# Loading x by channel halves in a long convolution by FFT: two alternating tiles, pieces behind the inverse evictions

## The chip, the cores and the metric

One Trainium2 chip, of which one core is used. The metric is the device time of one execution in microseconds (us). Three runs of the kernel before took 2089.24, 2091.68 and 2093.18 us; their median is 2091.68 us. One more execution was taken with the hardware profiler; all lines of the profile come from it.

A core has five engines, each with a queue of its own that runs in order: PE (matrix products; its weight loads are shown as PEld), DVE, ACT and POOL (elementwise work) and SP (it only issues transfers here). DMA transfers are issued from SP, ACT or POOL and run on 16 DMA engines that all of them share. A transfer that converts f32 to a 16 bit type is issued from POOL in this kernel.

## The reference

```python
def _attn_ref(x, h):                       # x: (8, 5696, 128), h: (5696, 128)
    L = 2 * S
    Xf = np.fft.rfft(x, n=L, axis=1)
    Hf = np.fft.rfft(h, n=L, axis=0)
    y = np.fft.irfft(Xf * Hf[None, :, :], n=L, axis=1)[:, :S, :]
    return y
def _moe_ref(x, w_theta, w_tok_r, w_tok_i, w_ch):
    theta = x @ w_theta
    zr, zi = x * np.cos(theta), x * np.sin(theta)
    y = einsum('ts,bsd->btd', w_tok_r, zr) + einsum('ts,bsd->btd', w_tok_i, zi)
    u = x + y
    return u + np.maximum(u @ w_ch, 0.0)
# reference(...) = _moe_ref(_attn_ref(x, h), ...)
```

A causal convolution over 5696 positions, for 8 batches and 128 channels, is computed by a Fourier transform of length 11392. Its result goes through a phase, two products with matrices of 5696 x 5696, and a channel product.

## The kernel before

The convolution comes first and ends some 420 us into the span; then two passes of products with the big matrices follow, with the weights streamed through a ring of six buffers (`load_w`, line 517, POOL), transposed by DVE (line 722) and multiplied by PE (line 1107).

The transform is split in two factors, 64 by 178 (`N2`, `N1`); 178 of real input needs `K1` = 90 frequencies. One *group* is two batches and 64 of the 128 channels (`HD`): `groups` has 8 of them, `(bp, dh)` with the batch pair `bp` 0 to 3 and the channel half `dh` 0 or 1, `dh` running fastest. A group goes through four stages:

- **Stage a** (`stage_a`, 16 chunks): four matmuls a chunk (line 195) with x as weights, then one eviction from PSUM to the tile `a`, on ACT (line 202; 0.69 us).
- **Stage b** (`stage_b`, 12 chunks, called forward chunks): `f2` (line 213) does the second factor with the table `w_t2`; ACT evicts to `xs` (line 310; 0.97 us); DVE multiplies by the spectrum of h into `uv` (lines 312 and 317; 1.23 us). The spectrum comes in tiles `hs` from `hf_hbm` (`load`, line 303, issued by SP): four buffers, so four chunks are loaded ahead and the others are issued as a product releases a buffer. After the last chunk 12 warm-up matmuls run (line 219).
- **Stage c** (`stage_c`, 16 chunks, the inverse's first factor): 16 matmuls a chunk (lines 333, 334), evicted to the tile `g`, mostly by DVE (line 341; 1.22 us), some by ACT (lines 338, 339).
- **Stage d** (`stage_d`, 7 chunks, the inverse's second factor): matmuls with `g` (line 356), evicted to `yt` by ACT or DVE (lines 362, 360), then stored to `yt_hbm` by SP (line 371).

All PSUM tiles of these stages come from one pool of four.

`woven` sorts the steps of several lists by a position between 0 and 1 and so fixes the order in which each engine gets them; a list spread from w0 to w1 has its step i of n at w0 + (i + 0.5)/n (w1 - w0). The loop over groups (from line 610) does two weaves for each group g. The first has stage c of g, stage a of g+1 and the first four `hs` loads of g+1. The second has stage b of g+1 and stage d of g. In the first, stage a lies between 0 and 0.35 when g has `dh` 0 and between 0 and 0.55 when it has `dh` 1; stage c lies between 0.06 and 1.

x is loaded by `load_x(bp)` (line 122): both channel halves of a batch pair at once, f32 to f16, in 16 transfers from POOL (line 131): for each of two batches and four ranges of 16 rows, one of 80 partitions and one of 9. There is one tile `x16` (pool `fft_x`, one buffer, row pitch `XP` = 132 elements). So the load of the next pair can go out when stage a of the second half has read the tile; `next_x` is put behind stage a in the first weave of each group with `dh` 0. The first pair is loaded at the start (line 234).

Before the groups, h is transformed the same way (lines 231 to 259). Meanwhile the tables are built in pieces: for 15 frequencies of `w_t2` at a time, `w_table` takes an iota and a scaling on POOL (lines 151, 153, two buffers), rounding on DVE (lines 156, 157, 164) and two sines on ACT (lines 161, 168). The pieces from 0, 15 and 30 are made before `load_x(0)`, those from 45, 60 and 75 after it. The h chunks 5 to 11 (`h_chunk`; evictions on line 247 for odd ones, on line 249 for even ones) need the later pieces. Then come the tables `r` (lines 276, 277), the signs (line 290) and `e`, also from POOL by way of DVE and ACT.

After the first weave of the seventh group, `xin` is closed: x's memory goes to the phase stage, and POOL loads `w_theta`, `w_ch` and the tile `ya` (lines 534 and 550), used from the last group's first weave on.

Of the kernel before, what the change touches and what calls it, by code (L numbers as in the profile page):

```python
# [12 lines left out]
F16 = mybir.dt.float16  # L13
# [9 lines left out]
def kernel(  # L23
# [10 lines left out]
    nc = tc.nc  # L34
    B, S, D = x.shape
    assert D == 128
    P = 128
# [39 lines left out]
    N2 = 64  # L77
    N1 = NF // N2
    NB = S // N2
    K1 = N1 // 2 + 1  # L80
    CK = 8
    HD = D // 2
    EN = N2 // 2 + 1
    WARM = 12
    XP = D + 4
    assert N1 * N2 == NF and NB * N2 == S and NB % 2 == 1 and K1 <= P
    CHK = [(c0, min(CK, K1 - c0)) for c0 in range(0, K1, CK)]
    NCK = len(CHK)
# [12 lines left out]
    conv, setup, xa, xin, pha = (ExitStack() for _ in range(5))  # L101

    def pool(name, bufs, stack, **kw):
        return stack.enter_context(tc.tile_pool(name=name, bufs=bufs, **kw))

    fa = pool("fft_a", 1, xa)
    fh = pool("fft_h", 4, xa)
    fx = pool("fft_x", 1, xin)
    NE, WB, BT = 9, 6 * 4 * CJ * 64, 7 * 1024
    keep = pool("keep", 1, ctx, side="right")  # L110
    fc = pool("fft_c", 1, conv, side="right")
# [8 lines left out]
    for p0, p1 in ((0, 80), (80, NB)):  # L120
        nc.gpsimd.dma_start(u_t[p0:p1, :N2 * D],
                            bass.AP(tensor=h.tensor, offset=h.offset + p0 * N2 * D,
                                    ap=[[N2 * D, p1 - p0], [1, N2 * D]]))

    def load_x(bp):
        x16 = fx.tile([P, 2, N2, XP], F16, tag="x16", name="x16")
        for e in range(2):
            src = x[2 * bp + e]
            for n0 in range(0, N2, 16):
                for p0, p1 in ((0, 80), (80, NB)):  # L130
                    nc.gpsimd.dma_start(  # L131
                        x16[p0:p1, e, n0:n0 + 16, :D],
                        bass.AP(tensor=src.tensor, offset=src.offset + (p0 * N2 + n0) * D,
                                ap=[[N2 * D, p1 - p0], [D, 16], [1, D]]))
        return x16

    lane = fc.tile([P, 2], F32)
    for p0 in (0, 64):
# [47 lines left out]
    def stage_a(lhs, both=False):  # L186

        st = {}

        def chunk(q):  # L190
            if q == 0:
                st["a"] = fa.tile([P, 2 * K1, HD], F16, tag="a", name="a_")
            ps = psum()
            for i in range(4):
                nc.tensor.matmul(ps[:, i // 2, (i % 2) * 2 * K1:(i % 2 + 1) * 2 * K1], lhs(q + i), f1_t[:NB],  # L195
                                 start=True, stop=True)
            a_out = st["a"][:, :, q:q + 4].rearrange("p k (a q) -> p k a q", a=2)
            a_in = ps[:, :, :4 * K1].rearrange("p a (q k) -> p k a q", q=2)
            if both and q % 8:
                nc.vector.tensor_copy(a_out, a_in)  # L200
            else:
                nc.scalar.activation(a_out, a_in, AF.Copy)
        return [lambda q=q: chunk(q) for q in range(0, HD, 4)], st
# [19 lines left out]
    def woven(*lists):  # L223

        lists = [l if isinstance(l, tuple) else (l, 0.0, 1.0) for l in lists]
        steps = [(w0 + (i + 0.5) / len(l) * (w1 - w0), n, f)
                 for n, (l, w0, w1) in enumerate(lists) for i, f in enumerate(l)]
        for _, _, f in sorted(steps, key=lambda s: s[:2]):
            f()
# [1 line left out]
    for k0 in (0, 15, 30):  # L231
        w_table(k0)
    nc.vector.tensor_copy(h16[:NB], u_t[:NB, :N2 * D].rearrange("p (n h d) -> p h n d", h=2, d=HD))
    x16s = {0: load_x(0)}
    steps, a_h = stage_a(lambda q: h16[:NB].rearrange("p h n d -> p (h n) d")[:, :, q], True)
    woven(steps, [lambda k0=k0: w_table(k0) for k0 in range(45, K1, 15)])

# [106 lines left out]
    def stage_d(st, bp, dh, then=None):  # L344
        def chunk(n0, cn):
            if n0 == 0:
                st["yt"] = fg.tile([P, NB, N2], BF16, tag="yt", name="yt")
            g_, yt = st["g"], st["yt"]
            ps = psum()
            nq = 5 if cn == CN else cn  # L350
            for j in range(cn):
                n = n0 + j
                o = ps[:, j // nq, (j % nq) * NB:(j % nq + 1) * NB]
                for ri in range(2):
                    e_ = e_t[:K1, n, ri, :] if n < EN else e_t[:K1, N2 - n, ri, ::-1]
                    nc.tensor.matmul(o, g_[:K1, ri * N2 + n, :], e_, start=(ri == 0), stop=(ri == 1))
            y_out = yt[:, :, n0:n0 + cn].rearrange("p m (a q) -> p m a q", q=nq)
            y_in = ps[:, :cn // nq, :nq * NB].rearrange("p a (q m) -> p m a q", q=nq)
            if n0 in (0, 3 * CN):
                nc.vector.tensor_copy(y_out, y_in)  # L360
            else:
                nc.scalar.activation(y_out, y_in, AF.Copy)
            if n0 + cn == N2:
                if then is not None:
                    then(yt)
                if then is not None:
                    gate = nc.gpsimd.tensor_copy(small(0, 1)[HD:HD + 1], sides["phases"][1][HD:HD + 1, 3, H - 1:H]).ins
                for e in range(2):
                    t0 = H if then else 0
                    with tc.issue_after(gate) if then else ExitStack():  # L370
                        (nc.gpsimd if then else nc.sync).dma_start(
                            yt_hbm[dh * HD:(dh + 1) * HD, 2 * bp + e, t0:],
                            yt[64 * e:64 * e + 64].rearrange("p m n -> p (m n)")[:, t0:])
        return [lambda n0=n0, cn=cn: chunk(n0, cn) for n0, cn in CHN]
# [4 lines left out]
    def front(g):  # L379
        if g >= len(groups):  # L380
            return [], [], []
        bp, dh = groups[g]
        x16 = x16s[bp].rearrange("p b n d -> p (b n) d")
        steps, a_st = stage_a(lambda q: x16[:NB, :, dh * HD + q])
        return (steps, *stage_b(a_st, dh))

    a0, load0, b0 = front(0)
# [222 lines left out]
    for g, (bp, dh) in enumerate(groups):  # L610
        st = {}
        last = g + 1 == len(groups)
        a_, load_, b_ = front(g + 1)
        if last:
            for _ in range(3):
                steps0.pop(0)()
        now = [with_load(steps0.pop(0), n < 6) for n in range(9)] if last else []
        c_ = stage_c(st, last)
        if dh == 0 and bp + 1 < B // 2:
            def next_x(bp=bp):  # L620
                x16s[bp + 1] = load_x(bp + 1)
            a_ = a_ + [next_x]
        woven((c_, 0.06 if a_ else 0.0, 1.0), (a_, 0.0, 0.35 if dh == 0 else 0.55), now, load_)
        if g + 2 == len(groups):
            xin.close()
            open_phases()
            load_ya0()
        now = [steps0.pop(0) for _ in range(5)] if last else []
        woven(b_, (stage_d(st, bp, dh, load_ya1 if last else None), 0.0, 1.1 if b_ else 1.0), now)
        if g + 2 == len(groups):  # L630
            load_ya1()
            open_ring()
# [56 lines left out]
    bp = cp = wlp = ybp = None  # L689
# [246 lines left out]
    nxt, second, st = None, None, {}  # L936
    ordered = ExitStack()
    for i, (k, p, tt, j0, s0, nj) in enumerate(stretches):
# [13 lines left out]
        if (p, tt, j0 + s0) == (0, 1, 0):  # L952
            with tc.issue_after(sides["late"].ins):
# [4 lines left out]
        woven = (tt is not None and end_of_pair and i + 1 < len(stretches)  # L958
                 and stretches[i + 1][2] is not None)
# [17 lines left out]
        if tt is None:  # L977
            if p:
                aside(True, False)
            if first_of_pair:  # L980
                q = M1 if p else M3
# [188 lines left out]
```

## Time and profile before

| What | Value |
|---|---|
| Profiled execution | 2090.45 us |
| Its span, first to last instruction | 2088.6 us |
| Mean granted TensorE clock | 0.977 |
| PE busy | 1970.4 us (94%) |
| DVE busy | 1589.4 us (76%) |
| POOL busy | 916.2 us (44%) |
| ACT busy | 646.7 us (31%) |
| DMA queue of POOL (software) | 272032 packets, 156.73 MB |
| DMA queue of SP and ACT (hardware) | 176096 packets, 164.05 MB |
| x transfers (line 131) | 32 of 320 KB (9.1 us to landing, median) and 32 of 36 KB (8.2 us) |
| hs transfers (line 303) | 192 of 128 KB, 3.2 us to landing, median |

How to read it. The page gives for each engine its busy time and share of the span. Other views show groups of instructions by source line, the waits of one engine for another, a timeline of one engine, and windows: the busy time of all engines in a stretch of the span, with the number of instructions in brackets, then the granted PE clock (1.00 is full speed), the mean busy share of the DMA engines (over 1 where packets of several queues overlap on one engine) and the GB/s written. In a timeline row stand the start, the duration, engine, line, operation, out<-in and the number of instructions merged, and in brackets the idle time before it with what ended it. A row of the waits has the total time in us, how often, and the longest.

### The profile page before, as it was taken

How to read it: one execution, taken by the hardware profiler on the slowest of the kernel's cores; microseconds unless marked ns; L12 is line 12 of the kernel's file. 1: busy time of each engine (PE TensorE's matmuls, PEld its weight loads, DVE VectorE, ACT ScalarE, POOL GpSimd, SP SyncE). 2: the span in 40 equal slices, each digit the busy share in tenths (PEclk: the TensorE clock that was granted, in tenths of full speed). 3: DMA queues.
4: the chain of work that ended last, by engine and by line, in shares of the span. 5: the costliest groups of instructions: out<-in, count | busy, mean ns of one | idle time of the engine just before them, and what ended most of it. 6: DMA issues, size and time to landing. Idle time of an engine off the chain costs nothing.

```text
span 2088.6 us, 41598 instructions
## 1 busy us (share of the span) xinstructions
PE 1970.4 (94%) x15865; PEld 1084.7 (52%) x15865; DVE 1589.4 (76%) x2809; ACT 646.7 (31%) x979; POOL 916.2 (44%) x1661
## 2 busy tenths in 40 slices
PE   4888989878999999999999999899999999999998
PEld 3687888754444444444444444344444444444444
DVE  7777768876778887888876766876867777777767
ACT  4877867773332323232310000011111111111111
POOL 5302021247444545454566554445353545444450
PEclk8799989999999999999999999999999999999999
DMA  9489595989898989898999899869697878878793
GB/s 142 102 138 172 146 147 164 249 248 244 145 162 172 180 169 168 171 179 171 177 171 163 130 197 258 135 115 154 127 154 128 153 133 146 145 136 151 131 154 86
DMA packets 454312, 334.98 MB, mean 160 GB/s; under 512 B 134823, under 2 KB 407335, under 8 KB 453127
## 3 DMA queue, kind: packets, MB, share of 16 engines
q0 software_dynamic: 272032, 156.73, 56.2%
q1 hardware_dynamic: 176096, 164.05, 27.3%
q10 hardware_dynamic: 5984, 11.54, 1.6%
q8 instruction: 124, 2.03, 0.4%
q14 instruction: 76, 0.62, 0.1%
HBM read 377.11 MB, written 92.49 MB: 225 GB/s over the span
## 4 chain that ended last, share of the span: by engine, by line
PE 65%; DVE 3%; DMA 2%; issue 1%; POOL 0%; ACT 0%; DVEq 0%; POOLq 0%
PE m L1107 61%; DMA ring<-in_moe_w_tok_r_dram 2%; DVE c L1114 1%; DVE b L663 1%; PE utp L802 1%; PE v L809 1%; PE m L1111 1%; DVE wt L722 1%; PE tpz L750 0%; PE theta_ps L404 0%; POOL ring L517 0%; PE m L994 0%; PE m L1028 0%; DMA zl<-zl_hbm 0%; DMA wl<-in_moe_w_tok_i_dram 0%
## 5 line engine op out<-in xcount | busy, mean ns | idle before, releaser
L517 POOL DMA_DIRECT2D ring<-in_moe_w_tok_i_dram x720 | 388.3, 547 | 660.4 <-DVE wt L722 587.5
L517 POOL DMA_DIRECT2D ring<-in_moe_w_tok_r_dram x720 | 386.4, 547 | 148.0 <-DVE wt L722 93.0
L722 DVE STREAM_TRANSPOSE wt<-ring 128x384 f32<-128x384 f32 (+2 forms) x720 | 360.2, 527 | 108.2 <-PE m L1107 70.9
L1107 PE MATMUL m<-b,wt 128*128 128x512 bf16 x1640 | 391.4, 381 | 2.0 <-DVE wt L722 1.7
L1107 PEld LDWEIGHTS <-wt 128*128 128x128 bf16 x1804 | 176.6, 98 | 220.3 <-DVE wt L722 7.5
L1114 DVE TENSOR_TENSOR c<-c,m 128x512 f32<-128x512 f32 x412 | 266.7, 673 | 0.4 <-PE m L1107 0.4
L804 ACT ACTIVATE ring<-utp 128x512 bf16<-128x512 bf16 x85 | 50.7, 597 | 582.1 <-PE utp L802 582.1
L312 DVE TENSOR_TENSOR uv_t<-xs,hs 128x2048 f16<-128x2048 f16 x88 | 105.6, 1224 | 34.9 <-ACT xs L310 20.1
L333 PE MATMUL ps<-r_u,uv_t 128*128 128x128 f16 x1024 | 122.4, 220 | 10.2 <-ACT red L427 3.5
L1028 PE MATMUL m<-b,wt 128*128 128x512 bf16 x480 | 113.9, 387 | 10.8 <-DMA b<-z_hbm 6.3
L131 POOL DMA_DIRECT2D x<-in_x_dram x64 | 48.5, 766 | 167.6 <-PE ps L195 156.7
L334 PE MATMUL ps<-r_v,uv_t 128*128 128x128 f16 x1024 | 121.5, 220 | 0.2
L799 ACT ACTIVATE ub<-c 128x512 bf16<-128x512 f32 x88 | 55.1, 628 | 193.1 <-DMA ring<-in_moe_w_tok_r_dram 114.4
L334 PEld LDWEIGHTS <-uv_t 128*128 128x128 f16 x1024 | 100.3, 98 | 9.3 <-issue 8.1
L333 PEld LDWEIGHTS <-uv_t 128*128 128x128 f16 x1024 | 100.5, 98 | 5.2 <-DVE uv_t L317 3.8
L310 ACT ACTIVATE xs<-ps 128x1024 f16<-128x1024 f32 x96 | 91.2, 986 | 33.1 <-PE ps L213 24.1
L1028 PEld LDWEIGHTS <-wt 128*128 128x128 bf16 x528 | 51.2, 99 | 71.7 <-issue 11.7
L213 PEld LDWEIGHTS <-w_t 64*128 64x128 f16 x3240 | 64.4, 105 | 42.2 <-issue 25.9
L406 ACT ACTIVATE red<-theta_ps,magic 128x512 f32<-128x512 f32 (+1 forms) x46 | 31.6, 687 | 133.1 <-PE theta_ps L404 101.9
L752 ACT ACTIVATE ring<-tpz 128x512 bf16<-128x512 bf16 (+1 forms) x46 | 27.5, 597 | 134.5 <-PE tpz L750 111.7
L428 ACT ACTIVATE mag<-mag,half_pi 128x512 f32<-128x512 f32 (+1 forms) x90 | 65.0, 723 | 0.0
L663 DVE TENSOR_TENSOR b<-b 128x1024 bf16<-128x1024 bf16 x100 | 61.5, 685 | 0.0
(2892 smaller groups left out, 3779.9 us busy)
## 6 DMA issues: line engine op xcount, KB each, us to landing
ring<-in_moe_w_tok_r_dram POOLq DMA_DIRECT2D x352, 96.0 KB, 4.4
ring<-in_moe_w_tok_i_dram POOLq DMA_DIRECT2D x352, 96.0 KB, 5.0
ring<-in_moe_w_tok_r_dram POOLq DMA_DIRECT2D x352, 80.0 KB, 4.3
ring<-in_moe_w_tok_i_dram POOLq DMA_DIRECT2D x352, 80.0 KB, 3.7
hs<-hf_hbm SPq DMA_DIRECT2D x192, 128.0 KB, 3.2
cp_hbm<-c SPq DMA_DIRECT2D x88, 256.0 KB, 2.4
c<-cp_hbm SPq DMA_DIRECT2D x88, 256.0 KB, 3.6
out_dram<-c SPq DMA_DIRECT2D x88, 256.0 KB, 4.2
```

The source lines that it names most:

```text
L213: nc.tensor.matmul(ps[:, e, j * HD:(j + 1) * HD], w_t2[rows, c0 + j, N2 * (1 - ri):N2 * (3 - ri)], a_st["a"][rows, ri * K1 + c0 + j, :], s ...
L310: nc.scalar.activation(xs[:, :, :, :ck], ps, AF.Copy)
L312: nc.vector.tensor_tensor(uv[:, :, :, c0:c0 + ck], xs.rearrange("p e d k -> p e (d k)").unsqueeze(1).to_broadcast([P, 2, 2, HD * CK]), hv. ...
L333: nc.tensor.matmul(o, u_t[:, at:at + P], r_u, start=True, stop=False)
L334: nc.tensor.matmul(o, v_t[:, at:at + P], r_v, start=False, stop=True)
L428: nc.scalar.activation(mag, mag, AF.Sin, bias=half_pi[:m], scale=-TWO_PI)
L517: nc.gpsimd.dma_start(wb[32 * i:32 * i + 32, :ng, :nj * 64], bass.AP(tensor=a.tensor, offset=a.offset + row0 * S + p * H + i * QR + j0 * 6 ...
L663: return [lambda f=f, x=x: f(*x) for f, x in ((nc.vector.tensor_sub, (bt[M3], b12, b22)), (nc.vector.tensor_sub, (bt[M4], b21, b11)), (nc. ...
L722: nc.vector.transpose(wt.rearrange("p j t r -> p (j t r)").bitcast(F32).rearrange("p (j g t) -> p g j t", j=TJ, g=4)[:, :ng, :nj], wb[:, : ...
L1028: nc.tensor.matmul(ms[n // 2 * 2 + h], a[n][:, j, :, r], bts_of[p][jj][n % 2 * 2 + h][:, r, :], start=(n % 2 == 0 and jj == 0 and r == 0), ...
L1107: nc.tensor.matmul(ms[q], a[q][:, j, :, r], bts[jj][q][:, r, :], start=(jj == 0 and r == 0), stop=(jj == NJ - 1 and r == 1 and q not in left))
L1114: nc.vector.tensor_tensor(c, z, ms[q], op=op)
```

## The change

`load_x` now takes a group number. It loads one channel half (64 of 128 channels, rows of 256 bytes in HBM instead of 512) into a tile of half the pitch (`XP` = 66), from a pool of two buffers. It gives back a list of eight pieces, each with a transfer of 80 partitions and one of 9. With `after`, a piece begins with a POOL copy of one element of the tile `g` into the place that the transfer will write, so that the transfer follows the eviction of inverse chunk 2i (element 16i). The pieces for group g+2 are woven into the first weave of group g, from 0.1 to 1.02. At the start the halves of groups 0 and 1 are issued one after the other. Stage a lies between 0 and 0.7 in every group. In the second weave stage d begins at 0.08 instead of 0, which puts its first chunk behind two forward chunks instead of one.

```diff
-    XP = D + 4
+    XP = HD + 2
...
-    fx = pool("fft_x", 1, xin)
+    fx = pool("fft_x", 2, xin)
...
-    def load_x(bp):
-        x16 = fx.tile([P, 2, N2, XP], F16, tag="x16", name="x16")
-        for e in range(2):
+    x16s = {}
+
+    def load_x(g, after=None):
+
+        bp, dh = divmod(g, 2)
+        if g >= B:
+            return []
+        if g not in x16s:
+            x16s[g] = fx.tile([P, 2, N2, XP], F16, tag="x16", name="x16")
+        x16 = x16s[g]
+
+        def piece(i):
+            e, n0 = i // 4, i % 4 * 16
             src = x[2 * bp + e]
-            for n0 in range(0, N2, 16):
-                for p0, p1 in ((0, 80), (80, NB)):
-                    nc.gpsimd.dma_start(
-                        x16[p0:p1, e, n0:n0 + 16, :D],
-                        bass.AP(tensor=src.tensor, offset=src.offset + (p0 * N2 + n0) * D,
-                                ap=[[N2 * D, p1 - p0], [D, 16], [1, D]]))
-        return x16
+            if after is not None:
+                g_ = after["g"]
+                nc.gpsimd.tensor_copy(x16[0:1, e, n0, 0:1], g_[0:1, 0, 16 * i:16 * i + 1])
+            for p0, p1 in ((0, 80), (80, NB)):
+                nc.gpsimd.dma_start(
+                    x16[p0:p1, e, n0:n0 + 16, :HD],
+                    bass.AP(tensor=src.tensor, offset=src.offset + (p0 * N2 + n0) * D + dh * HD,
+                            ap=[[N2 * D, p1 - p0], [D, 16], [1, HD]]))
+        return [lambda i=i: piece(i) for i in range(8)]
...
-    x16s = {0: load_x(0)}
+    for f in load_x(0) + load_x(1):
+        f()
...
-        x16 = x16s[bp].rearrange("p b n d -> p (b n) d")
-        steps, a_st = stage_a(lambda q: x16[:NB, :, dh * HD + q])
+        x16 = x16s[g].rearrange("p b n d -> p (b n) d")
+        steps, a_st = stage_a(lambda q: x16[:NB, :, q])
...
-        if dh == 0 and bp + 1 < B // 2:
-            def next_x(bp=bp):
-                x16s[bp + 1] = load_x(bp + 1)
-            a_ = a_ + [next_x]
-        woven((c_, 0.06 if a_ else 0.0, 1.0), (a_, 0.0, 0.35 if dh == 0 else 0.55), now, load_)
+        woven((c_, 0.06 if a_ else 0.0, 1.0), (a_, 0.0, 0.7), now, load_, (load_x(g + 2, st), 0.1, 1.02))
...
-        woven(b_, (stage_d(st, bp, dh, load_ya1 if last else None), 0.0, 1.1 if b_ else 1.0), now)
+        woven(b_, (stage_d(st, bp, dh, load_ya1 if last else None), 0.08 if b_ else 0.0, 1.1 if b_ else 1.0), now)
```

## The prediction

> **What bounds the kernel now.** The page's chain of waits gives 61% of the span to the matmuls of line 1107, the weight stage after the convolution. None of them changes, so the change is worth what it moves the end of the convolution, which lies in the first 420 us; all that follows starts when its data is there and moves with it. I take the convolution's groups apart by the stretches between their PE landmarks: c(g) runs from the end of one warm-up (line 219) to the next first matmul of line 213, b(g+1) from there to the next warm-up's end. c holds the inverse chunks of group g woven with stage a of group g+1, b the forward chunks of g+1 woven with stage d of g. Windows at these boundaries, c0, b1, c1, b2 and so on:
>
> ```profile
> core 0: us, PE busy (x) PEld busy (x) DVE busy (x) ACT busy (x) POOL busy (x), PEclk, DMA share, GB/s
> 84.54:107.35 22.81, 20.56 (x322) 19.49 (x321) 16.12 (x16) 16.66 (x26) 9.27 (x13) 1.00 0.86 124
> 107.35:129.44 22.09, 16.23 (x499) 14.09 (x498) 16.00 (x14) 14.32 (x16) 2.83 (x4) 0.85 1.26 174
> 129.44:149.34 19.90, 19.90 (x328) 19.64 (x325) 14.63 (x14) 16.46 (x26) 0.00 (x0) 1.00 0.44 122
> 149.34:165.69 16.35, 14.44 (x499) 12.54 (x498) 14.20 (x13) 13.45 (x16) 0.00 (x0) 1.00 0.39 114
> 165.69:189.32 23.63, 21.03 (x328) 19.91 (x326) 15.91 (x15) 17.01 (x27) 8.98 (x12) 1.00 1.06 178
> 189.32:212.37 23.05, 16.94 (x499) 14.93 (x498) 16.13 (x14) 14.38 (x16) 3.00 (x4) 0.85 1.26 168
> 212.37:232.28 19.91, 19.91 (x328) 19.64 (x325) 14.49 (x14) 16.47 (x26) 0.00 (x0) 1.00 0.46 121
> 232.28:248.62 16.34, 14.38 (x498) 12.45 (x497) 14.76 (x13) 13.77 (x16) 0.00 (x0) 1.00 0.39 117
> 248.62:271.23 22.61, 20.81 (x330) 19.82 (x327) 15.34 (x15) 16.54 (x27) 8.84 (x12) 1.00 1.04 179
> 271.23:296.76 25.53, 19.23 (x498) 16.63 (x497) 16.39 (x14) 14.68 (x16) 3.13 (x5) 0.73 1.15 166
> 296.76:316.67 19.91, 19.91 (x328) 19.65 (x326) 14.21 (x13) 16.47 (x26) 0.00 (x0) 1.00 0.42 108
> 316.67:333.01 16.34, 14.52 (x498) 12.52 (x497) 15.02 (x13) 13.76 (x16) 0.00 (x0) 1.00 0.43 124
> 333.01:354.94 21.93, 20.57 (x330) 19.75 (x327) 15.17 (x17) 16.57 (x27) 5.49 (x9) 1.00 0.76 225
> 354.94:371.27 16.33, 14.26 (x498) 12.49 (x497) 14.37 (x13) 13.70 (x16) 0.32 (x1) 1.00 0.55 164
> ```
>
> Two kinds stand out. Three of the b stretches (22.09, 23.05, 25.53) are longer than the other four (16.33 to 16.35), with a DMA share over 1.1 and a granted clock of 0.73 to 0.85 where the others have 1.00. And c with an even group takes 21.93 to 23.63, with an odd one 19.90, in which PE has no gap at all. What DVE waits for in these groups says the first:
>
> ```profile
> DVE uv_t L312 <- ACT xs L310: 14.6, 32, 2.3
> DVE uv_t L312 <- DMA hs<-hf_hbm: 14.3, 10, 3.0
> ```
>
> In the long b stretches the spectra (hs) are late, because the whole next x pair is loaded then: POOL issues it once stage a has read the tile (at 96.6, 178.6 and 260.9), and the last transfer lands some 13 us into b.
>
> **The b stretches, price of the stall.** If x is out of the way they should take 16.34: (22.09-16.34) + (23.05-16.34) + (25.53-16.34) = 5.75 + 6.71 + 9.19 = **21.65 us gained**. The lower clock there goes with it, as it follows the holes in PE.
>
> **The new x load: is it out of the way?** Each group now loads half a pair behind its own inverse evictions. Piece i waits for chunk 2i; by the weave's positions these end near 0.09 + 0.117i of c, so pieces go out every 2.35 us, the last near 19 us into c of 20. The number of rows stays, each is half as long, so the packets double over the kernel. x alone has this rate:
>
> ```profile
> 27.00:32.00 5.00, 3.38 (x120) 3.22 (x120) 4.93 (x7) 2.34 (x3) 4.72 (x8) 1.00 1.70 164
> ```
>
> 164 GB/s written, so a whole pair (2.92 MB in f16) takes 17.8 us when alone. A half load is not in this trace. From below it is 8.9 us (price by bytes), from above 17.8 (price by packets). Between them: the software queue's packets lasted 43 ns for x (542 engine-us of 12,544 packets, 167 to 213 us) and 75 ns for the rings of 1280 and 1536 byte reads (2885 engine-us of 38,298, 1600 to 1900 us); a line through 512 bytes at 43 and 1408 at 75 gives 34 at 256, or 0.79 of 17.8 = **14.0 us**, which I take. That is 1.75 us a piece, below the 2.35 between pieces, so the load keeps pace and ends 2 to 4 us into b. Before, 13 us of overlap cost 7.2 us on average, 0.55 for each, but the first two forward chunks have their hs already (four are loaded ahead), so I put **0.5 us for each of six b stretches (b1 to b6), 3 us lost**. Ends: 0, and 2.5 each (15) if a half costs 17.8 and shares the engines with hs.
>
> The Trainium skill speaks against the halves: DMA: Bandwidth & Descriptors, section Specifications, asks for at least 512 B a transfer for line rate and says that below it the DMA engine does read-modify-write. The 256 B written here already moved 164 GB/s, so the row does not show a wall at that size; by the rule a half would cost a whole, and the sum below would end near 2090. The same page (Why small descriptors are slow) counts 3 cycles of overhead a packet, 11 cycles for 256 B against 19 for 512 by its formula, an estimate of 0.58 of a pair, with which the sum would be 2 us lower than mine.
>
> **The c stretches.** Even groups wove stage a into the first 0.35 of c: 2.7 stage-a chunks to an inverse chunk, and ACT, which evicts them at 0.69 us each (1.86 in all, PE 1.76), set the pace; then inverse chunks alone at DVE's 1.22. At 0.7 there are 1.34 stage-a chunks to one inverse chunk: ACT 0.92, DVE 1.22, PE 0.89 + 1.34 x 0.325 = 1.33 us, so PE is the bound as in the odd groups now. Only two stage-a chunks instead of three then cover the wait for the last uv product, 0.3 us. I take 20.2 for all seven: 7 x 20.2 = 141.4 against 150.7 now, **9.3 us gained**; ends 19.9 (11.4) and 20.8 (5.1).
>
> **Stage d's start.** The first d chunk goes behind two forward chunks. Now it sits behind one and waits for the last inverse eviction, and ACT with it:
>
> ```profile
> 152.48 1.94 ACT L310 ACTIVATE xs<-ps 128x1024 f16<-128x1024 f32 x2 [1.43 <-PE ps L213]
> ```
>
> The 1.43 us come back only as far as DVE, 14.2 to 15.0 busy of 16.3, does not bound the rest: 0.4 in each of seven, **2.8 us gained**; ends 0 and 1.2 each (8.4).
>
> **The start, where the change costs.** Before, 12 of the first 16 x transfers stand on POOL between the table step at 22.87 and the tables from k=45 on; in the changed program's order 27 stand there, since group 1's half is issued at once too, and a half needs as many descriptors as a whole. POOL and then DVE:
>
> ```profile
> 22.87 1.06 POOL L153 TENSOR_SCALAR turn<-whole,lane 128x960 f32<-128x960 f32 x1
> 23.99 7.71 POOL L131 DMA_DIRECT2D x<-in_x_dram  x10
> 31.98 1.50 POOL L131 DMA_DIRECT2D x<-in_x_dram  x2 [0.28 <-DMA x<-in_x_dram]
> 33.48 1.97 POOL L151 IOTA whole<- 128x960 f32 x2
> 35.55 2.23 POOL L153 TENSOR_SCALAR turn<-whole,lane 128x960 f32<-128x960 f32 x2
> ```
>
> The first of the two turn steps ends at 36.7 and DVE takes it at 37.45, so 0.8 us is slack. Behind DVE's line 156 stand the odd h chunks from 5 on (line 247), r, sign and e tables; ACT's sines and PE's h chunks 5 to 11 wait for the same tables, and stage a of group 0 is behind them on PE. DVE was busy for nearly all of this stretch, so nothing gives the time back. Issue-bound, 27 x 0.77 = 20.8 us from 24.0: x done at 44.8, 11.3 later, **10.5 us** after slack. But by the program's waits each x transfer is held until the one eight before it has landed; at 1.75 us a pair the first four pairs go at 1.53 and 9.5 at 1.75: 22.7, x done at 46.7, 13.2 late, **12.4 us lost**, which I take. At the whole's price, 2.2 us a pair: 27.0, so 16.7 lost.
>
> **At nothing.** 48 gate copies: a copy of one element took 0.18 us on POOL, which stood idle for 67 us between loads; uncovered they would be 8.6. The pieces of 9 partitions are not gated and go early; POOL has room. Weight loads with a row pitch of 132 instead of 264 bytes: x took 157 ns, h with 128 bytes 172, both under matmuls; uncovered 15 ns x 64 = 1 us a group. The load of ya (line 550) waits for stage a of group 7, which ends near 14 us into c6 instead of 12, and had landed by 359 for a use after 371: 10 us of cover.
>
> **Sum.** The profiled execution took 2090.45 us (span 2088.6), 1.2 under the median of the runs, 2091.68. 2090.45 - 21.65 + 3 - 9.3 - 2.8 + 12.4 = 2072.1; as a median, **2073**. With the best ends -11.4 - 21.65 - 8.4 + 10.5 = -31: 2061. With the worst -5.1 - 21.65 + 15 + 16.7 = +5: 2097.
>
> **Rivals.**
> 1. *The start hides the extra transfers*: the tables still come in time, so 12.4 is not lost: 2061. For it: POOL idles at 39.3 to 42.3. Against: the turn step has 0.8 us of slack. 0.10.
> 2. *Slower: half packets cost as much as whole ones and x runs into every b.* A whole pair took 24.5 us beside hs (178.6 to 203); so a half ends 2.3 + 24.5 = 26.8 after c began, 6.6 us into b, at 0.55 that is 3.6 each, 21.8 in six; the start 16.7; no gain by d: 2091.7 - 21.65 - 9.3 + 21.8 + 16.7 = 2099. It decides from 2.4 us for each b on. For it: packets far below 1 KB, DMA share 1.26 under x now. Against: 164 GB/s written, 328 read, looks like bytes rather than packets. 0.13.
> 3. *Half the gain in c and b stays away*: stage a stretched to 0.7 leaves DVE at 1.22 of 1.33 us with four PSUM buffers, so c stays near 21, and hs waits cost 1 us each: 2073 + 7 x 0.8 + 6 x 0.5 = 2082. 0.15.
> That the load stays in one burst I exclude: each piece of 80 partitions carries its gate in the program's order.
>
> **How the numbers follow.** Forecast 0.62 (own range 2063 to 2086), rivals 0.10, 0.13, 0.15. A measurement of this kernel tells 0.2% (4.2 us) from no change: under 2087.5 is faster, over 2095.9 slower. Faster: 0.58 + 0.10 + 0.13 = 0.81; same 0.03 + 0.03 + 0.02 = 0.08; slower 0.01 + 0.10 = 0.11. The range for 8 in 10: 2060 to 2093.
>
> **What would show it.** b1, b3, b5 at 16 to 17 us with granted clock 1.00, few DVE waits on hs; b2, b4, b6 no longer than 17; all c at 20 to 20.5; the two iotas for k=45 and 60 near 46 instead of 33.5, and group 0's first forward chunk near 80 instead of 67.6. I am wrong if b2 or b4 exceed 19 (rival 2), if c0 starts by 86 (rival 1), or if the convolution's gain is gone by the end.

## The result and the profile after

| | Before | Changed |
|---|---|---|
| Median of 20 runs each | 2090.31 us | 2083.89 us |
| Ratio to the kernel before, 95% interval | | 0.9971 [0.9962, 0.9981] |
| Profiled execution (span) | 2090.45 (2088.6) us | 2088.55 (2086.7) us |
| Second profile of each (span) | 2095.55 (2093.7) us | 2088.18 (2086.4) us |

The change makes the kernel 6.4 us faster; the forecast was 18.7. Single executions of one kernel spread over some 11 us (2079.2 to 2090.96 for the changed one), and the profiled one of the changed kernel lies 4.7 us above its median. Terms are therefore read below from stretches of the convolution, in two profiles where there are two, and totals from the ratios. As kernels were timed in several sessions, whose medians of the kernel before lie between 2090.31 and 2093.81 us, ratios are compared and not medians.

The windows of the changed kernel at the boundaries used in the prediction (c0, b1, c1, b2, c3, b4, c6, b7; columns as there):

```profile
95.60:121.33 25.73, 22.52 (x320) 22.12 (x318) 17.56 (x17) 18.04 (x28) 9.44 (x18) 0.87 0.79 91
121.33:138.79 17.46, 14.55 (x499) 12.82 (x498) 14.78 (x13) 14.08 (x16) 3.91 (x7) 1.00 0.88 152
138.79:161.15 22.36, 20.29 (x328) 19.71 (x327) 15.42 (x15) 16.52 (x27) 9.44 (x18) 1.00 1.16 156
161.15:178.60 17.45, 14.38 (x498) 12.59 (x497) 15.13 (x14) 14.18 (x16) 3.91 (x7) 1.00 0.91 154
...
217.52:237.83 20.31, 20.16 (x329) 19.71 (x327) 14.18 (x14) 16.30 (x26) 9.45 (x18) 1.00 1.32 168
237.83:257.04 19.21, 16.06 (x499) 13.57 (x497) 16.32 (x14) 14.21 (x16) 3.89 (x7) 0.91 0.89 157
...
332.76:353.54 20.78, 20.16 (x328) 19.70 (x326) 15.30 (x18) 16.38 (x27) 3.92 (x6) 1.00 0.63 165
353.54:376.07 22.53, 17.29 (x499) 14.49 (x497) 16.26 (x14) 14.21 (x16) 1.27 (x2) 0.85 0.73 220
```

The long b stretches of before (22 to 25.5) are gone, and none of the new ones with x under way is near them. But their floor is 17.45 and not 16.34; c0 (25.73) and b7 (22.53) are long; and c as a whole has not become shorter. In us, before against changed:

| Stretch | Before | Changed | Difference | Forecast |
|---|---|---|---|---|
| Start of the first forward chunk | 67.58 | 79.03 | +11.45 | +12.4 |
| b1 to b7 | 136.0 | 129.7 | -6.3 | -21.45 |
| c0 to c6 | 150.7 | 150.7 | 0.0 | -9.3 |
| The rest, by difference | | | -7.05 | 0 |
| Profiled execution | 2090.45 | 2088.55 | -1.9 | -18.35 |

(-21.45 is -21.65 + 3 - 2.8.) Some 5.3 of the rest lie between the end of the convolution and about 600 us, see the last section. The second profiles of the two kernels give +9.3 for the start, -10.6 for b and +4.8 for c. How the change divides between b and c thus differs from run to run, but b and c together fall by 6.3 and 5.8, where 30.75 were forecast.

Of the signs named in the prediction, group 0's first forward chunk is where it should be (79.03), but b2, b4 and b6 are not within 17, and b4 is over the 19 that stood for the second rival. The second profile has 17.94 for b4, and the run without later x below has one b of 18.99, so this is not that rival.

The waits of PE between 84 and 380 us (total, how often, longest), first before, then changed. "issue" is a wait for nothing that the profile shows:

```profile
PE ps L213 <- issue: 10.4, 6, 3.8
PE ps L356 <- issue: 5.8, 4, 4.0
PE ps L333 <- DVE uv_t L317: 2.4, 3, 1.2
```

```profile
PE ps L369 <- ACT xs L323: 10.0, 16, 1.5
PE ps L225 <- issue: 5.5, 7, 1.7
PE ps L346 <- DVE uv_t L330: 4.9, 4, 3.2
```

The lines moved by 12 or 13: 225 are the forward matmuls, 346 the first inverse ones, 369 those of stage d. The two rows without a visible cause, 16.2 us, became one of 5.5 (and smaller ones of 2.8 and 1.2); in their place PE waits 10.0 us in stage d for PSUM that ACT's xs evictions release, and twice as long for the last uv product.

### The profile page after: what moved, and what is told of

Its sections match the earlier page's. It is cut to its first block, busy times and chain, and to the rows that moved or that the text cites. A ratio compares the mean times of both kernels' runs of the same rounds, so it can differ in the third digit from the quotient of the medians.

```text
span 2086.7 us, 41598 instructions
## 1 busy us (share of the span) xinstructions
PE 1955.1 (94%) x15688; PEld 1083.5 (52%) x15865; DVE 1587.1 (76%) x2809; ACT 646.6 (31%) x979; POOL 972.5 (47%) x1773
## 3 DMA queue, kind: packets, MB, share of 16 engines
q8 instruction: 124, 2.03, 0.4%
## 4 chain that ended last, share of the span: by engine, by line
PE 62%; DVE 4%; DMA 2%; issue 2%; POOL 1%; ACT 0%; DVEq 0%; POOLq 0%
PE m L1116 58%; DVE c L1123 2%; POOL ring L530 1%; DMA ring<-in_moe_w_tok_r_dram 1%; DVE b L672 1%; PE utp L811 1%; PE v L818 1%; PE m L1120 1%; DVE wt L731 1%; PE theta_ps L417 0%; PE tpz L759 0%; DMA wl<-in_moe_w_tok_i_dram 0%; PE m L1003 0%; DMA yT<-yt_hbm 0%; PE m L1037 0%
## 5 line engine op out<-in xcount | busy, mean ns | idle before, releaser
L1116 PE MATMUL m<-b,wt 128*128 128x512 bf16 x1599 | 386.1, 380 | 4.1 <-DVE wt L731 1.7
L346 PE MATMUL ps<-r_u,uv_t 128*128 128x128 f16 x1024 | 127.7, 221 | 7.7 <-DVE uv_t L330 4.9
L347 PE MATMUL ps<-r_v,uv_t 128*128 128x128 f16 x1024 | 126.6, 221 | 1.6 <-issue 1.2
L1037 PE MATMUL m<-b,wt 128*128 128x512 bf16 x466 | 111.8, 386 | 8.9 <-DMA b<-z_hbm 4.3
L143 POOL DMA_DIRECT2D x<-in_x_dram x128 | 96.9, 762 | 25.4 <-POOL x L141 12.6
L419 ACT ACTIVATE red<-theta_ps,magic 128x512 f32<-128x512 f32 (+1 forms) x46 | 31.6, 687 | 136.9 <-PE theta_ps L417 107.2
```

Source lines behind the costliest of these rows:

```text
L143: nc.gpsimd.dma_start(x16[p0:p1, e, n0:n0 + 16, :HD], bass.AP(tensor=src.tensor, offset=src.offset + (p0 * N2 + n0) * D + dh * HD, ap=[[N2 ...
L346: nc.tensor.matmul(o, u_t[:, at:at + P], r_u, start=True, stop=False)
L347: nc.tensor.matmul(o, v_t[:, at:at + P], r_v, start=False, stop=True)
L1037: nc.tensor.matmul(ms[n // 2 * 2 + h], a[n][:, j, :, r], bts_of[p][jj][n % 2 * 2 + h][:, r, :], start=(n % 2 == 0 and jj == 0 and r == 0), ...
L1116: nc.tensor.matmul(ms[q], a[q][:, j, :, r], bts[jj][q][:, r, :], start=(jj == 0 and r == 0), stop=(jj == NJ - 1 and r == 1 and q not in left))
```

## The experiments

Each has one profile. A ratio is that of its runs to runs of the kernel before in the same session. "Changed" is the kernel of the diff. In the cuts `...` stands for what is the same on both sides.

**Stage d back at 0.0.**

```diff
-        woven(b_, (stage_d(...), 0.08 if b_ else 0.0, 1.1 if b_ else 1.0), now)
+        woven(b_, (stage_d(...), 0.0, 1.1 if b_ else 1.0), now)
```

> The changed kernel, with stage d starting at 0 again instead of 0.08; all else as changed. Theory A (the later start of stage d itself lengthens b: in the profile after, four b stretches take 17.45 us to the hundredth, with PE's d matmuls waiting for PSUM tiles that ACT's xs evictions release): b1, b2, b5, b6 come back to 16.3 to 16.5, seven times 1.1, so 7 to 8 us below the changed kernel, ratio to the kernel before 0.993 to 0.995. Theory B (the 17.45 comes from spectra that are late behind the tail of the x load): b stays at 17.4 or more, and the time goes up by up to 3 us, ratio 0.997 to 0.999, since PE and ACT wait for d0 again.

Measured: 0.9989 [0.9977, 1.0002], against 0.9971 for the changed kernel. b2 returned to 16.34 and the sum of b1 to b7 fell from 129.7 to 125.3, but c rose from 150.7 to 156.6. Of the 4.4 that b saves only 1.3 lie in b1 to b6, the rest in b7; c more than pays them back.

**Group 1's x woven into the first forward stage.**

```diff
-    for f in load_x(0) + load_x(1):
+    for f in load_x(0):
...
-    woven(b0, [lambda n0=n0: e_table(n0) for n0 in range(0, EN, 11)])
+    woven(b0, [lambda n0=n0: e_table(n0) for n0 in range(0, EN, 11)], (load_x(1), 0.2, 0.8))
```

> The changed kernel, with the half of group 1 issued not at the start but woven into the first stage b, among the e tables; all else as changed. Theory A (27 transfers ahead of the tables on POOL delay the whole start, as forecast and as the profile after shows: the two iotas at 44.8 instead of 33.5): group 0's first forward chunk comes back from 79.0 to 67.5 to 69, all after it 11 us earlier, ratio to the kernel before 0.990 to 0.993. Theory B (what follows the convolution takes up a shift of the convolution in part: in the profile after, the convolution ends 4 us later than before, the span 2 us earlier): the convolution ends 11 us earlier, the span only 4 to 6: ratio 0.994 to 0.996.

Measured: 0.9923 [0.9908, 0.9938]; the first forward chunk begins at 67.06 instead of 79.03. The gain over the changed kernel, 0.0048 or 10 us, is near the 12.4 forecast for the start: it is the largest single loss of the change.

**The last stage a within 0.35, so that ya is loaded earlier.**

```diff
-        woven((c_, ...), (a_, 0.0, 0.7), ...)
+        woven((c_, ...), (a_, 0.0, 0.35 if g == 6 else 0.7), ...)
```

> The changed kernel, with stage a of the last forward group (in c6) between 0 and 0.35 as in the kernel before; all else as changed. Theory A (b7 takes 22.5 instead of 16.3 because stage a now ends later, so that POOL issues the loads of ya later and their transfers run into b7's spectra): the first load of ya goes out 3 to 4 us earlier within c6, b7 takes 16.3 to 18, c6 1 us more; 3 to 5 us below the changed kernel, ratio to the kernel before 0.994 to 0.9955. Theory B (b7 is long through the start of stage d or something else that is not ya): b7 stays at 21 to 23, the time within 1.5 us of the changed kernel, ratio 0.997 to 0.998.

Measured: b7 17.45 instead of 22.53, so the later end of stage a, and with it the load of ya behind it, is what lengthened it. In the total it doesn't show: 0.9963 [0.9950, 0.9976], and c2 and c3 of its profile took 23.19 and 21.21 instead of 20.73 and 20.31.

**Stage a within 0.35 and 0.55, as before.**

```diff
-        woven((c_, ...), (a_, 0.0, 0.7), ...)
+        woven((c_, ...), (a_, 0.0, 0.35 if dh == 0 else 0.55), ...)
```

> The changed kernel, with stage a between 0 and 0.35 for groups with dh 0 and between 0 and 0.55 for dh 1, as before; all else as changed. Theory A (the wide spread itself gains about 1.5 us in each even c, and loses at the start of c0 and c1, where only two stage-a chunks cover the wait for the last uv product and PE's clock falls): c2, c4 and c6 go from 20.2 to 20.8 up to 21.9 to 22.5, c0 comes down from 25.7 to 23, b7 to 17 or 18 as the loads of ya go out earlier; the time within 3 us of the changed kernel, ratio 0.995 to 0.998. Theory B (as forecast, the wide spread is worth 9 us): 7 to 9 us slower than the changed kernel, ratio 1.000 to 1.002.

Measured: 0.9997 [0.9983, 1.0011]. The wide spread of stage a is worth 0.0026 (5.4 us), more than half of the 9.3 forecast, but the profile doesn't show it where it was forecast: c is 151.5 in sum instead of 150.7. b7 falls to 17.46, as ya is loaded earlier, and b1 to b6 take 112.9 instead of 107.2, with b2, b3 and b5 at 18.75 and b4 at 21.28. c2 and c4, with stage a in the first 0.35, take 21.35 each, c1, c3 and c5 20.16 to 20.53; so the spread has a part of about 1 us in an even c.

**The two kernels once more.** 

> The kernel before once more, for a second profile. If the stretches of one profile are typical, b1, b3 and b5 take 21 to 26 us, with one gap of PE of 3 to 4 us each, c with odd groups 19.9, and the stretch from the last stage d to 600 us behaves as in the first profile. If chance has a large part in it, b1, b3, b5 differ by 2 us and more between the two, and the time from the last stage d to 600 us by 4 us and more.

> The changed kernel once more, for a second profile and timed on the same chip as the three others. Ratio to the kernel before 0.995 to 0.998. Where stretches of the first profile differ by more than 1 us from this one (c1 22.4, c2 20.7, b4 19.2, b7 22.5), chance decides them; the four b stretches of 17.45 and the start (first forward chunk at 79) should be the same.

Measured: b1, b3, b5 of before again long (26.45, 21.92, 24.04) and c1, c3, c5 again 19.90 to 19.97; the changed kernel again with 17.46 as the floor of b, c0 at 25.74 and b7 at 21.61, but c5 and c6 at 23.6 and 23.3 instead of 20.6 and 20.8. So c0, the floor and b7 belong to the kernel, and single c stretches of 23 us to the run.

**No x loads behind the first two groups.** All later groups read the x of groups 0 and 1; the loading of six halves and their gate copies are left out.

```diff
+        if after is not None:
+            x16s[g] = x16s[g - 2]
+            return []
```

> The changed kernel without the x loads and gate copies of groups 2 to 7: these groups transform the x of groups 0 and 1 again, so the output is not the reference's; all else as changed. Theory A (the x transfers, spread as they are, still delay PE's instruction fetches and the spectra): PE's gaps of over 0.7 us at the boundaries of 128 weight load and matmul pairs go away in c1 to b6, c1 to c5 take 20.1 to 20.4, b1 to b6 17.45 each (or less); 5 to 9 us below the changed kernel, ratio to the kernel before 0.993 to 0.995. Theory B (x is out of the way as forecast, and the c and b stretches are longer for the order of PE's work alone): c1 to c5 and b1 to b6 stay as they are, at 20.2 to 22 and 17.45 to 19; within 2 us of the changed kernel.

Measured: 0.9971 [0.9956, 0.9985], the same as with all loads. So x, spread behind the inverse evictions, costs nothing that can be seen in the total. b1 to c6 take 230.5 us in its profile, against 232.2 with the loads. The floor of b stays at 17.45. c0 is 21.34, behind a first forward stage that is 1.3 us longer: the wait at the start of c0 is 1.16 us instead of 3.2, and 0.8 us of c0 run at half the clock instead of 6.8. Whether x has a part in that is open. In the changed kernel the small transfers of group 2's x, which have no gate, are issued in that forward stage.

**Both repairs: group 1's x late, the last stage a within 0.35.** The edits of the second and third experiment together.

> The changed kernel with both repairs: group 1's half is woven into the first stage b, and stage a of the last forward group ends at 0.35 of c6. If the gains of the two add: 10 to 11 us of the one, 0 to 4 of the other, ratio to the kernel before 0.990 to 0.992, first forward chunk at 67 to 68, b7 at 17.5. If they do not add since what follows the convolution sets the end: 0.992 to 0.994.

Measured: 2070.7 us, 0.9906 [0.9889, 0.9923], the fastest that was run and faster than both kernels; the changed one had 0.9965 in the same session. The next two experiments and the last one start from this version.

**The same with stage d at 0.0.** Edit as in the first experiment.

> The version with both repairs (group 1's x woven into the first forward stage, last stage a within 0.35; 2070.7 us) with stage d back at 0.0 in the second weave, the third part of the change alone taken back, now without the start and ya in the way. The prediction's term (the later start of d gains 0.4 us in each of seven stretches) says 2070.7 + 2.8 = 2073.5. The rival read from the b floors (17.45 with d at 0.08, 16.34 with d at 0.0, 7 x 1.11 us) says 2070.7 - 7.8 = 2063. A second rival, from the earlier run with stage d at 0.0 (4 us slower than the changed kernel although its b2 was 16.34): what b saves comes back as waits in c, 2070 to 2076, with a sum of b1 to b7 of 116 to 121 and a sum of c of 155 or more instead of 149.6.

Measured: 0.9923 [0.9903, 0.9942]. Sum of b1 to b7 121.4 instead of 125.3, of c 158.5 instead of 149.6: the second rival. Two pairs of windows, b2 and c2, b4 and c4, first with stage d at 0.08 (the kernel with both repairs), then at 0.0:

```profile
148.43:165.88 17.45, 14.53 (x498) 12.72 (x497) 15.42 (x14) 14.17 (x16) 3.90 (x7) 1.00 0.91 154
165.88:186.31 20.43, 20.17 (x329) 19.71 (x326) 14.79 (x14) 16.34 (x27) 9.45 (x18) 1.00 1.35 172
...
224.54:241.99 17.45, 14.71 (x499) 12.75 (x498) 15.43 (x14) 14.07 (x16) 3.91 (x7) 1.00 0.90 154
241.99:262.44 20.45, 20.16 (x328) 19.70 (x326) 14.81 (x14) 16.34 (x27) 9.46 (x18) 1.00 1.24 172
```

```profile
150.54:166.88 16.34, 14.57 (x498) 12.52 (x497) 14.65 (x13) 13.76 (x16) 3.92 (x7) 1.00 0.94 155
166.88:188.20 21.32, 20.16 (x329) 19.70 (x326) 15.65 (x15) 16.71 (x27) 9.45 (x18) 1.00 1.23 172
...
228.53:245.87 17.34, 14.30 (x498) 12.34 (x497) 13.88 (x12) 14.33 (x16) 3.90 (x7) 1.00 0.90 145
245.87:269.72 23.85, 21.79 (x330) 21.33 (x327) 16.39 (x15) 16.26 (x26) 9.45 (x18) 0.93 1.08 154
```

With d at 0.0, PE waits some 1 us into c, for the last uv product or for a PSUM tile that ACT has not yet evicted: 1.09 us in c2, 1.99 in c4. Behind the short wait the clock stays at 1.00, behind the long one it is 0.93 on average, and the pair takes 41.2 us; the other takes 37.7. With d at 0.08 the same two pairs take 37.9 us each, and no wait at the start of these c is as long as 0.4. So the later stage d moves a wait from the start of c, where it can cost the clock, into b. In the total the two pairs of kernels differ by 0.0018 and 0.0017 in the same direction, each within its intervals.

**Stage a of group 1 begun earlier.** Four stage-a chunks instead of two ahead of c0's first inverse chunk.

```diff
-        woven((c_, ...), (a_, 0.0, 0.35 if g == 6 else 0.7), ...)
+        woven((c_, ...), (a_, -0.1 if g == 0 else 0.0, 0.35 if g == 6 else 0.7), ...)
```

> Same version (2070.7 us, d at 0.08), with stage a of group 1 begun at -0.1 instead of 0.0 in the first weave, so that four stage-a chunks instead of two stand on PE before the first inverse chunk of group 0. Theory: c0 is long (25.9 us, against 20.2 to 21.4 for the others) because PE runs out of stage-a work and waits 3.2 us for the last uv product, and the granted clock is 0.50 for some 4 to 7 us behind this gap; two more chunks cover about 1.3 us and keep the gap under 2 us: c0 22 to 23.5, total 2067 to 2068.5. Rival: the wait only moves (stage a's PSUM tiles are taken, ACT is late as well), c0 stays at 25 to 26, total 2070 to 2072.

Measured: 0.9914 [0.9895, 0.9933], c0 25.45. The wait of 3.2 us became two, of 0.67 and 1.30, but the granted clock in c0 stayed at 0.87. More cover by real work didn't help; the rival was right on c0. c2, which the edit doesn't touch, took 24.67 behind a wait of 2.83 us in this profile.

**The kernel before without the x of pairs 1 to 3.**

```diff
-                x16s[bp + 1] = load_x(bp + 1)
+                x16s[bp + 1] = x16s[bp]
```

> The kernel before without the x loads of batch pairs 1 to 3: all groups read the x of pair 0 (this leaves out the loading of six of the eight groups' x, 16 of 16 transfers for each of three pairs). Prices the first term of the prediction by itself: if the long b1, b3 and b5 come from the x burst (late hs, and PE's own instruction fetches late behind it), these become 16.34 and the kernel gains about 21.65 us, less what even c stretches give: 2068 to 2071. Rival: part of the long b's is not x (order of stages, ACT), then b1, b3, b5 stay above 18 and the gain is under 12 us. For the stretch between the last stage d and 600 us: 187 as before if x has no part in it, 180 to 182 as in the changed kernels if a quiet convolution is what shortens it.

Measured: 0.9925 [0.9905, 0.9944]. Its windows b1 and c1, b3 and c3, b5 and c5, and the first three rows of PE's waits:

```profile
107.87:124.54 16.67, 14.52 (x498) 12.43 (x497) 14.60 (x13) 13.26 (x16) 0.00 (x0) 1.00 0.44 121
124.54:146.47 21.93, 20.30 (x330) 19.82 (x327) 15.77 (x15) 17.40 (x28) 0.00 (x0) 1.00 0.47 124
...
185.28:201.90 16.62, 14.48 (x498) 12.37 (x497) 14.06 (x13) 12.71 (x15) 0.00 (x0) 1.00 0.39 113
201.90:225.72 23.82, 22.03 (x328) 21.51 (x326) 16.41 (x15) 17.93 (x28) 0.00 (x0) 0.93 0.46 119
...
265.52:282.14 16.62, 14.26 (x498) 12.47 (x497) 14.34 (x13) 12.99 (x15) 0.00 (x0) 1.00 0.43 117
282.14:304.15 22.01, 20.42 (x329) 19.90 (x325) 16.12 (x15) 17.66 (x28) 0.00 (x0) 1.00 0.46 126
```

```profile
PE ps L333 <- DVE uv_t L317: 6.1, 8, 1.2
PE ps L213 <- DVE yt L360: 3.7, 6, 1.0
PE ps L213 <- issue: 3.3, 7, 0.9
```

This is the run that explains most. b1, b3 and b5 together fall from 70.67 to 49.91, 20.8 us: the price of the stall was right, and it was x. But c1, c3 and c5, which had no gap in PE at all, rise from 59.74 to 67.76, 8.0 us, although nothing in them was touched: 5.0 are idle time of PE, and 1.7 the lower clock in c3. PE's waits for uv go from 2.4 to 6.1 us. c2, c4 and c6, with stage a in the first 0.35, take 22.4 to 22.5 here, so without the long b even and odd c are nearly alike.

**More warm-up matmuls behind group 0's forward chunks.** 28 instead of 12, useless work in the hole at the start of c0.

```diff
+    warms = [12, 28] + [12] * 7
...
-            for n in range(WARM):
+            for n in range(warms.pop(0)):
```

> The version with both repairs (2070.7 us) with 28 instead of 12 warm-up matmuls behind the forward chunks of group 0 alone: 16 more useless matmuls of about 0.16 us, 2.6 us of PE work laid into the 3.2 us in which PE waits for the last uv product at the start of c0. Theory: what makes c0 long is not the wait itself but the granted clock that falls to 0.50 behind it (the clock changes on a grid of 3.413 us, and a window in which PE stood still for more than about 1.3 to 2 us is followed by one at half speed); with the hole filled the clock stays at 1.00, b0 becomes 18.9 to 19.2, c0 20.5 to 22 instead of 25.9, the pair b0 + c0 39.5 to 41 instead of 42.25, and the total 2068 to 2070. Rival: ACT's last eviction, or DVE and ACT as such, set the pace there, and the longer warm-up pushes them back: the pair stays at 42 to 45 and the total at 2070 to 2074, whatever the clock does.

Measured: c0 20.06 instead of 25.91, b0 and c0 together 39.91 instead of 42.25. Windows over the start of c0, first with 12 warm-ups, then with 28:

```profile
82.00:86.00 4.00, 1.91 (x14) 1.20 (x11) 4.00 (x4) 3.80 (x4) 0.00 (x0) 0.93 0.56 164
86.00:90.00 4.00, 2.35 (x21) 2.29 (x22) 2.04 (x5) 1.76 (x4) 0.00 (x0) 0.50 0.55 164
90.00:94.00 4.00, 4.00 (x45) 4.00 (x44) 2.44 (x3) 2.20 (x3) 1.11 (x2) 0.66 0.35 78
```

```profile
82.00:86.00 4.00, 4.00 (x21) 2.12 (x20) 4.00 (x5) 3.22 (x4) 0.00 (x0) 0.75 0.59 169
86.00:90.00 4.00, 3.67 (x53) 3.42 (x52) 2.61 (x5) 2.51 (x4) 0.00 (x0) 1.00 0.59 167
90.00:94.00 4.00, 4.00 (x67) 4.00 (x66) 3.76 (x4) 2.98 (x5) 2.18 (x4) 1.00 0.72 76
```

With 12, PE is busy for 1.91 of 4 us in the first window, and from 86 on it gets half the clock for about 6.8 us. With 28 it is kept busy, and the clock is at 1.00 from 84 on. Of the 5.85 us by which c0 is shorter, 3.5 are only moved into b0, where the warm-ups now fill the wait; the 2.3 us left are the lower clock. They are not seen in the total (0.9910 [0.9892, 0.9927] against 0.9906): c2 took 23.18 in this profile, behind a wait of 1.34 us.

## Why the prediction was wrong in size

**The step that failed** is the pair "If x is out of the way they should take 16.34 [...] 21.65 us gained" and "I take 20.2 for all seven [...] 9.3 us gained". Both numbers occur in the profile of before, but never next to each other: a c of 19.9 always followed a long b, and a b of 16.34 was always followed by a c of 21.9 to 23.6. I read the difference between even and odd c as the effect of stage a's spread. The kernel before without later x shows that it is mostly what precedes: while PE stands in a long b, DVE and ACT catch up, and c starts without waiting (c1, c3 and c5 of before have no idle time of PE). When b runs at its floor, the uv products lag behind PE, c begins with a wait, and where this wait is long the granted clock falls too. So of the 20.8 us that the stalls cost, 8.0 come back in c. The undisturbed pair (b and the c behind it) was 38.3 to 40.0 in before. It is 38.0 to 39.8 in the changed kernel from b1 on, where the sum of the prediction has 36.6. In none of the 14 profiles did any of these pairs take less than 37.67.

Term by term, with the changed kernel's first profile:

- **Start, 12.4 lost: right in size, by two errors that offset each other.** 11.45 in the first profiles (9.3 in the second), and undoing it (the second experiment) gives about 10 back. The sum had x 13.2 later on POOL, less 0.8 of slack. POOL's rows show the step, the two iotas for k=45 and 60 at 44.84 where 33.48 stood: 11.36 later, as in the smaller, issue-bound case of the prediction, and no slack in between:

```profile
22.23 1.06 POOL L165 TENSOR_SCALAR turn<-whole,lane 128x960 f32<-128x960 f32 x1
23.36 17.28 POOL L143 DMA_DIRECT2D x<-in_x_dram  x23
41.01 1.50 POOL L143 DMA_DIRECT2D x<-in_x_dram  x2 [0.37 <-DMA x<-in_x_dram]
43.34 1.50 POOL L143 DMA_DIRECT2D x<-in_x_dram  x2 [0.83 <-DMA x<-in_x_dram]
44.84 1.97 POOL L163 IOTA whole<- 128x960 f32 x2
```

- **The stall of the long b, 21.65: right in price** (20.8 without later x), but late spectra are only a part of it: PE's holes without a visible cause in these b, 16.2 us, are another (last section).
- **The tail of x in b, 3 lost: too much, if anything.** Without any later x the changed kernel has the same total. The packets of a half lasted 30.4 ns on average (12,544 of them between 138 and 180 us) against 43 for a whole; the prediction took 34. The Trainium skill (DMA: Bandwidth & Descriptors, Specifications) asks for 512 B and more for line rate; reads of 256 B instead of 512 cost nothing visible here, as the load has a whole c to spread over.
- **Stage d's start, 2.8 gained: probably the right sign, by another mechanism.** b didn't get shorter by 0.4, its floor rose by 1.11 (16.34 to 17.45, stage d's matmuls waiting for PSUM from ACT). The gain is in c, whose first wait shrinks. Undoing it costs about 3.6 us twice, each time within the intervals, so the sign is not shown by the totals.
- **b1 to b6** were forecast at 16.44 each, 98.6 together, and took 107.2: 8.6 of the miss. **c1 to c6** were forecast at 121.2 and took 125.0: 3.8.
- **c0, forecast 20.2, took 25.73: 5.5.** The wait for the last uv product is 3.2 us there and not 0.3; pieces of the e table stand between the products on DVE and ACT, as they did in before. Behind it 6.8 us run at half the clock, 3.4 us lost. Two stage-a chunks stand ahead of the first inverse chunk instead of four, but the two runs with four (stage a as before, stage a of group 1 earlier) have 25.5 as well, so the cover is not what decides. I had taken c0 for a stretch like the others.
- **"The load of ya [...] 10 us of cover": wrong, 6.6 us in b7** (22.53, forecast 15.94). I asked whether ya lands in time for its own use and not what else is on the DMA engines then. Stage a ends later, ya is issued at 349 to 358, and b7's spectra are late. In DVE's rows the wait of 3.59 us names them:

```profile
361.53 1.23 DVE L325 TENSOR_TENSOR uv_t<-xs,hs 128x2048 f16<-128x2048 f16 x1 [0.49 <-ACT xs L323]
366.35 1.22 DVE L325 TENSOR_TENSOR uv_t<-xs,hs 128x2048 f16<-128x2048 f16 x1 [3.59 <-DMA hs<-hf_hbm]
```

- 8.6 + 3.8 + 5.5 + 6.6 = 24.5 us too little in b and c; the start gave 1 back, and about 7 came from a part of the kernel that I had at nothing. That leaves the 16.5 by which the profiled execution missed the sum.

Of the rivals, the third (half of the gain in c and b stays away, 2082) came closest to the measured 2083.89, but by luck: the cause that it gave, a c that stays near 21 and 1 us of late spectra in each b, is not what happened (most c behind c0 are at 20.2 to 20.8, and b is long by PE's waits in stage d, without later x as well). The second, whole price for half packets, is out: no x at all changes nothing. That the start hides the extra transfers is out too.

## What to carry to other kernels

Two stretches that follow each other on the same engines have one floor together: before a stall is counted as gain, look whether the next stretch was short because of it, and compare pairs and not the best of each. When a load is spread so that it fits, look also at what was queued behind the step that now ends later, and at whose transfers it meets, even if it is in time for its own use. Transfers that are moved to the start of a kernel were paid in full here, as the issuing engine also makes the tables.

## What the runs showed of the hardware

**The clock goes by slots.** In all profiles the granted PE clock changes only on a grid of 3.413 us, whose phase against the kernel differs from run to run, and it is 1.00 or 0.50 in a slot; in the convolution it stays low for one to three slots as a rule (five at most). I counted over 14 profiles, from 84 to 640 us, all slots at full clock by how long PE had no matmul in them:

| PE idle in a slot | Slots | Followed by a slot at 0.50 |
|---|---|---|
| under 1.2 us | 1698 | 2 |
| 1.2 to 1.6 | 79 | 14 |
| 1.6 to 2.0 | 47 | 22 |
| 2.0 to 2.2 | 17 | 16 |
| over 2.2 | 46 | 46 |

So a hole of 1.3 to 2 us costs nothing more, or up to 1.7 us (half a slot, an estimate) for each slot that the clock stays low, depending on how it falls on the grid. This fits the single c of 23 us that come and go, and makes holes under about 1.2 us the aim. The Trainium skill (TensorE: Matmul & The Clock Gate, Part 1) describes this free-running window of 3413 ns, and the records agree; its section "Why this matters for your kernels" asks only for no gaps over some 3 us, and here ones of 1.2 to 2 us were enough in 36 of 126 slots.

**PE stands still without a visible cause under x.** The waits marked "issue" in before lie at equal distances: in b1 at pair 92 of 128 LDWEIGHTS and MATMUL pairs, twice; in b3 at 89, twice; in b5 at 86, twice. 128 pairs are 256 instructions, and the instruction queue moved 2.03 MB in 124 packets, 16 KB each. The longest of these holes lie inside the x burst:

```profile
116.39 0.76 PE L213 MATMUL ps<-a__1342,w_t 64*128 64x64 f16 x21 [3.83 <-issue]
...
198.80 1.20 PE L356 MATMUL ps<-e_t,g__3368 90*128 90x89 f16 x20 [3.97 <-issue]
...
282.29 1.88 PE L213 MATMUL ps<-a__5344,w_t 64*128 64x64 f16 x63 [3.70 <-issue]
```

Without the later x of before the longest is 0.9. In each of the three a packet of the instruction queue was under way (113.42 to 114.86, 195.76 to 197.20, 279.35 to 280.62): it started 0.8 to 0.9 us after PE had stopped, and PE went on 1.5 to 1.7 us after it ended. I infer that PE waited for its next packet of instructions behind x; no run tried the fetch by itself. So the long b's were probably not only late spectra.

**Not settled.** From the end of the convolution to about 600 us, two profiles of before took 187.2 and 187.0 us and the changed kernel 181.9 and 179.9; its variants lie between 180.0 and 185.2, and before without later x at 184.4. All that follows the convolution took 1668.8 and 1668.7 us in before, 1662.7 and 1660.4 in the changed kernel, so the difference arises in this part. In part it is the clock: a PE wait of 1.73 us near 572 us stands in all of them, and only in the three with x loaded by pairs did the clock fall behind it. Nothing in the change is meant for this part, and no run isolated it. Why c0 is not helped by four stage-a chunks ahead of it, and why it is short in the run without later x, is open as well.
